# Two units of layer 2 run ahead in the scores' banks, block 1's last units move in front of block 0's last sums, and layer 2's seven products add up in PSUM

## The chip, the cores and the metric

One core of one Trainium2 chip runs the whole kernel. The metric is the device time of one execution in microseconds. PE is the matrix engine (TensorE), DVE is VectorE, ACT is ScalarE, SP issues nearly all DMAs.

## What is computed

Three parts in a row, on 4 x 576 = 2304 tokens of width 512 (8 heads of 64), all in fp32 or better:

```python
scores = q @ k.T / sqrt(64); causal softmax; local = a @ v
mem = (phi(q) @ M_prev) / (phi(q) . z_prev + 1e-6)     # phi(x) = elu(x) + 1
x = sigmoid(beta) * mem + (1 - sigmoid(beta)) * local   # attention
x = softplus(x @ w_in) @ w_out                          # layer 1, 512 -> 2048 -> 512
out = relu(x @ w2_in)**2 @ w2_out                       # layer 2, 512 -> 2048 -> 512
```

The weights arrive as float64. Products run on 16-bit halves: each fp32 operand is split into a high and a low part, and one product is three matmuls (high x high, high x low, low x high).

## The kernel before

**Tiling and order.** Attention goes through 18 chunks g of 128 tokens, 8 heads each, in 104 steps (`attn_step`): scores into the two-bank tile `s_ps` (line 342), mask and row maximum on DVE (line 347), exp on ACT (351), split and transpose, then P x V (399) four steps later. Layer 1 goes through 9 blocks kb of 256 tokens (two chunks). Its work is cut into units: `unit_h(kb, fp)` makes 256 of 2048 hidden columns (24 matmuls, lines 502 to 504; softplus on ACT and DVE, lines 506 to 513, result g in two halves), `unit_x(kb, cp, f0, f1)` the second product (lines 519 to 521) for two of four output chunks over hidden chunks f0 to f1. Block 0 uses `unit_xq(0, q)` instead (lines 564 to 566), which adds quarter q of the hidden chunks into two PSUM banks `xacc` held for the whole block. `w` units split one weight piece (lines 480 to 490).

**What sets the order.** The program is written out in order, and a scheduler with a modelled time puts each engine's instructions in a fixed order, by priority (attention's ones raised) and readiness; every engine then works through its list in order. The planner (lines 692 to 740) mixes units into the attention steps: while the attention of block kb runs, it writes out units of earlier blocks up to `lim`, the modelled time of the queue less a reserve `LEAD_NS` (line 700); `unit_time` (654) prices a unit by its matmuls. Line 717 onward builds the queue for block 1: after three quarters of block 0, six h units of block 1 and their partial sums over f 0 to 12 run early; then come h(0,6), h(0,7), xq(0,3), `close` (which ends the pools `mma`, `xac` and `stage`), h(1,6), h(1,7) and the rest of the sums. The tiles g are named by fp, one buffer each.

**After attention** (lines 742 to 767) the rest of the queue runs while layer 2's weights are loaded and split (`w34_to`), then all PSUM pools close and `mm2` opens with eight banks.

**Layer 2.** The first 512 tokens go the plain way: `plain_h(j)` makes 16 chunks of 128 hidden columns (12 matmuls of 512 columns each, lines 793 to 795), `row_tile` the second product (988 to 990). The other seven blocks of 256 tokens (kb = 2 to 8) use seven products in place of eight for a 2x2 block product. `sums_w3` and `sums_w4` make the sums of weight quarters on DVE, `x_parts(kb)` those of the input. `seven_h(kb, q)` makes half of the hidden columns from seven products of 24 matmuls of 128 columns (878 to 880), each in a bank of its own; DVE adds them up in SBUF (886 to 895), ACT applies Relu and Square. `parts` splits the result, `seven_o(kb, which)` does the second product the same way (938 to 940, adds in line 944), `plain_o` without the trick for two blocks. The results of `seven_h(kb, 0)` lie in the upper half of W3 (`RB`), so they can only be written once `sums_w3` has read it.

**Lines touched:** 161 and 583 (buffers of z and of keys 1), 510 (names of g), 700, 735 to 737 (planner), 761 to 772 (the end of layer 1 and the pools), 783 to 802, 868 to 897, 930 to 964, 997 to 1016, 1027 to 1031.

Of the kernel before, what the change touches and what calls it, by code (L numbers as in the profile page):

```python
# [17 lines left out]
P = 128  # L18

LAG = 4  # L20
LEAD_NS = 15000.0
FR = 0.4
# [33 lines left out]
def kernel(  # L56
# [103 lines left out]
    def z_setup():  # L160
        zr = stage.tile([B * H, 2, D], F32, name="zr", bufs=1)
        z16 = stage.tile([B * H, 2, 2, D], F16, name="z16", bufs=1)
        for i in range(2):
            act.dma_start(out=zr[:, i], in_=z_prev.rearrange("b h d -> (b h) d"))
        act.activation(z16[:, 0], zr, AF.Copy)
        dve.tensor_tensor(z16[:, 1], zr, z16[:, 0], ALU.subtract)
        ps = mm.tile([P, 2, B * H], F16, tag="mm", name="zps")
        for t in range(2):
            pe.transpose(ps[:, t], z16[:, t].rearrange("p i d -> p (i d)"), ident[:B * H, :B * H])
        act.activation(zc, ps, AF.Copy)  # L170
# [321 lines left out]
    g_t = {}  # L492

    def unit_h(kb, fp):
# [15 lines left out]
        g = [w1p.tile([P, 2, NB], F16, name=f"g{t}_{fp}") for t in range(2)]  # L510
# [68 lines left out]
    load("k", 1, stage)  # L579
# [116 lines left out]
    for kb in range(1, NBLK + 1):  # L696
        if kb == 1:
            lim = FR * sum(unit_time(u) for u in queue)
        else:
            lim = sum(unit_time(u) for u in queue) - LEAD_NS  # L700
# [16 lines left out]
        if kb == 1:  # L717
            done = 4 - sum(u[0] == "xq" for u in queue)
            if done < 4:
# [14 lines left out]
                queue = out_q + early + [("close",)]  # L734
                if done < 4:
                    new = new[nh:]
                    xs = [("x", kb, c, 2 * nh, NFC) for c in range(NCC // 2)]
# [22 lines left out]

    for n_, u in enumerate(queue):
        run_unit(u)
        w34_to(NPC * (n_ + 1) // nu)
    mm_cm.__exit__(None, None, None)
    pv_cm.__exit__(None, None, None)
    sps_cm.__exit__(None, None, None)
# [5 lines left out]
    mm2 = ctx.enter_context(tc.tile_pool(name="mm2", bufs=8, space=PSUM, reuse_waits="tile"))  # L772
# [10 lines left out]
    def plain_h(j):  # L783
        x = x_t[0]
        new_g(j)
        for h in range(2):
            for i in range(2):
                f = h * HF + j + i
                ps = mm2.tile([P, 512], F32, tag="mm2", name="h2ps")
                for c in range(NCC):  # L790
                    wh, wl = (w[:, c, f * P:(f + 1) * P] for w in W3)
                    xh, xl = (x[:, t * NCC + c] for t in range(2))
                    pe.matmul(ps, wh, xh, start=(c == 0), stop=False)
                    pe.matmul(ps, wh, xl, start=False, stop=False)
                    pe.matmul(ps, wl, xh, start=False, stop=(c == NCC - 1))
# [5 lines left out]
                dve.tensor_copy(hi, r)  # L801
# [66 lines left out]
    def seven_h(kb, q):  # L868
        X = XT[kb % 2]

        def prod(w, x):
            ps = mm2.tile([P, 512], F32, tag="mm2", name="h2ps")
            for i in range(4):
                o = ps[:, i * P:(i + 1) * P]
                for k in range(2):
                    wh, wl = w3_at(w, k, 4 * q + i)
                    xh, xl = (y[:, x, k * P:(k + 1) * P] for y in X)
                    pe.matmul(o, wh, xh, start=(k == 0), stop=False)  # L878
                    pe.matmul(o, wh, xl, start=False, stop=False)  # L879
                    pe.matmul(o, wl, xh, start=False, stop=(k == 1))  # L880
            return ps.rearrange("p (j t) -> p j t", j=4)
# [3 lines left out]
        act.activation(r11, prod(0, 0), AF.Copy)  # L885
        dve.tensor_tensor(r12, prod(3, 4), r11, ALU.add)
        dve.tensor_tensor(r22, prod(4, 5), r12, ALU.add)
        dve.tensor_tensor(r21, prod(2, 6), r22, ALU.add)
        p5 = prod(6, 3)
        dve.tensor_tensor(r22, p5, r22, ALU.add)  # L890
        dve.tensor_tensor(r12, p5, r12, ALU.add)
        act.activation(r[1], r[1], AF.Relu, scale=u2)
        act.activation(r[1], r[1], AF.Square)
        dve.tensor_tensor(r11, prod(1, 1), r11, ALU.add)
        dve.tensor_tensor(r12, prod(5, 2), r12, ALU.add)
# [29 lines left out]
    OB = {}  # L925

# [3 lines left out]
    def seven_o(kb, which):  # L930
        def prod(n):
            gi, wi = PR[n]
            ps = mm2.tile([P, 512], F32, tag="mm2", name="ops")[:, :256]
            for j in range(HF):
# [3 lines left out]
                pe.matmul(ps, gh, wh, start=(j == 0), stop=False)  # L938
                pe.matmul(ps, gh, wl, start=False, stop=False)  # L939
                pe.matmul(ps, gl, wh, start=False, stop=(j == HF - 1))  # L940
            return ps

        def add(o, ps, y):
            dve.scalar_tensor_tensor(o, ps, SO, y, ALU.mult, ALU.add)

        if which == 0:
            OB[kb] = TS[:, :, NB:]
        o = OB[kb]
        o11, o12, o21, o22 = (o[:, i] for i in range(4))
        if which == 0:  # L950
            act.activation(o12, prod(6), AF.Copy, scale=SO)
            add(o21, prod(7), o12)
            p5 = prod(5)
            add(o22, p5, o21)
            add(o12, p5, o12)
            add(o12, prod(3), o12)
            return
        p1 = prod(1)
        act.activation(o11, p1, AF.Copy, scale=SO)
        add(o[:, 1:], p1.rearrange("p (a c) -> p a c", a=1).to_broadcast([P, 3, 256]), o[:, 1:])  # L960
        add(o11, prod(2), o11)
        store(2 * kb, o[:, :2])
        add(o21, prod(4), o21)
# [33 lines left out]
    for j in range(0, HF, 2):  # L997
        plain_h(j)
        w34_to(NPC + 2 * j + 4)
    st2_cm.__exit__(None, None, None)  # L1000
# [14 lines left out]
    for m in range(XB // P):  # L1015
        row_tile(0, m, XB // 2)
    for j in W4A:
        sums_w4(j)
# [8 lines left out]
    for kb in range(K0, NBLK):  # L1027
# [3 lines left out]
        seven_h(kb, 0)  # L1031
# [41 lines left out]
```

## Time and profile before

| | |
|---|---|
| median of 3 runs | 943.59 us (941.1 to 945.34) |
| the profiled execution | 943.42 us, span 941.6 us |
| mean granted PE clock | 0.979 |
| PE busy | 880.2 us, 93% |
| DVE busy | 728.3 us, 77% |
| ACT busy | 613.6 us, 65% |
| DMA queue 1 | 53.3% of 16 engines |

Times in the rows count from the start of the span. A busy PE is not PE at its peak, as matmuls are pipelined. The granted clock is a share of 2.4 GHz: 0.50 is 1.2 GHz. "Idle before, releaser" at the end of a row is how long the engine stood before that instruction and what ended the wait.

### The profile page before, as it was taken

How to read it: one execution, taken by the hardware profiler on the slowest of the kernel's cores; microseconds unless marked ns; L12 is line 12 of the kernel's file. 1: busy time of each engine (PE TensorE's matmuls, PEld its weight loads, DVE VectorE, ACT ScalarE, POOL GpSimd, SP SyncE). 2: the span in 40 equal slices, each digit the busy share in tenths (PEclk: the TensorE clock that was granted, in tenths of full speed). 3: DMA queues.
4: the chain of work that ended last, by engine and by line, in shares of the span. 5: the costliest groups of instructions: out<-in, count | busy, mean ns of one | idle time of the engine just before them, and what ended most of it. 6: DMA issues, size and time to landing. Idle time of an engine off the chain costs nothing.

```text
span 941.6 us, 24682 instructions
## 1 busy us (share of the span) xinstructions
PE 880.2 (93%) x10385; PEld 730.7 (78%) x10394; DVE 728.3 (77%) x1474; ACT 613.6 (65%) x1160; POOL 2.2 (0%) x10
## 2 busy tenths in 40 slices
PE   5757999889999898999999999999999999999997
PEld 3346888679878897899988887444776999999983
DVE  6798999878757676667856699999997998767640
ACT  7977688679769695867958375663266656444530
POOL 0000000000000000000000000000000000000000
PEclk9879899899999999999999999999999999999999
DMA  9999998799876978658845666500000000000001
GB/s 234 205 217 203 223 206 177 133 150 150 130 131 117 144 134 127 116 101 131 136 86 75 171 199 182 178 22 23 24 2 24 2 24 1 25 24 2 24 13 34
DMA packets 285023, 101.24 MB, mean 108 GB/s; under 512 B 248048, under 2 KB 284400, under 8 KB 284912
## 3 DMA queue, kind: packets, MB, share of 16 engines
q1 hardware_dynamic: 284672, 99.65, 53.3%
q8 instruction: 81, 1.33, 0.6%
q14 instruction: 30, 0.25, 0.1%
q10 hardware_dynamic: 240, 0.02, 0.0%
HBM read 48.78 MB, written 4.72 MB: 57 GB/s over the span
## 4 chain that ended last, share of the span: by engine, by line
PE 52%; DVE 22%; ACT 10%; DMA 10%; issue 5%; SPq 0%; ACTq 0%; DVEq 0%
PE h2ps L878 4%; PE h2ps L879 4%; PE h2ps L880 4%; PE hps L503 4%; PE hps L502 4%; DMA rawq<-in_q_dram 4%; PE hps L504 4%; DMA PT<-p 3%; PE ops L940 3%; PE ops L938 3%; PE ops L939 3%; DVE wcv L481 3%; PE s_ps L342 3%; PE xps L520 3%; PE xps L519 3%
## 5 line engine op out<-in xcount | busy, mean ns | idle before, releaser
L502 PE MATMUL hps<-x,W 128*128 128x256 f16 x576 | 157.5, 275 | 3.8 <-DVE spa L509 1.8
L503 PE MATMUL hps<-x,W 128*128 128x256 f16 x576 | 158.1, 275 | 0.5 <-ACT x L545 0.4
L504 PE MATMUL hps<-x,W 128*128 128x256 f16 x576 | 157.8, 275 | 0.0
L520 PE MATMUL xps<-g,W 128*128 128x256 f16 x512 | 138.8, 273 | 2.4 <-DVE g L513 2.4
L519 PE MATMUL xps<-g,W 128*128 128x256 f16 x512 | 137.8, 273 | 3.3 <-ACT g L512 3.3
L521 PE MATMUL xps<-g,W 128*128 128x256 f16 x512 | 138.8, 273 | 0.0
L351 ACT ACTIVATE Pt<-Pt,cs 128x128 f32<-128x128 f32 (+4 forms) x144 | 84.6, 588 | 45.1 <-DVE cs L347 45.0
L342 PE MATMUL s_ps<-KT,qT 128*128 128x128 f16 (+2 forms) x992 | 75.4, 219 | 22.1 <-DVE cs L347 20.8
L375 DVE TENSOR_TENSOR p<-Pt,p 128x512 f16<-128x512 f32 (+2 forms) x100 | 66.5, 665 | 30.0 <-ACT p L374 29.8
L342 PEld LDWEIGHTS <-qT 128*128 128x128 f16 (+1 forms) x992 | 56.2, 103 | 40.3 <-issue 32.6
L347 DVE CUSTOM_DVE_ANT_0 Pt<-s_ps,mask 128x128 f32<-128x128 f32 (+3 forms) x128 | 61.8, 483 | 19.5 <-PE s_ps L342 19.2
L374 ACT ACTIVATE p<-Pt 128x512 f16<-128x512 f32 (+2 forms) x100 | 60.5, 605 | 15.0 <-DMA PT<-p 14.1
L503 PEld LDWEIGHTS <-W 128*128 128x128 f16 x576 | 56.8, 99 | 9.6 <-issue 3.4
L502 PEld LDWEIGHTS <-W 128*128 128x128 f16 x576 | 56.9, 99 | 7.7 <-DVE spa L509 1.1
L504 PEld LDWEIGHTS <-W 128*128 128x128 bf16 x576 | 56.8, 99 | 7.2 <-issue 0.8
L399 PE MATMUL pvt<-V,PT 128*128 128x64 f16 (+1 forms) x1392 | 58.8, 196 | 1.3 <-DMA PT<-p 1.3
L513 DVE TENSOR_TENSOR g<-spa,g 128x512 f16<-128x512 f32 x72 | 49.4, 685 | 11.2 <-ACT g L512 11.0
L509 DVE SCALAR_TENSOR_TENSOR spa<-hps,spa 128x512 f32<-128x512 f32 x72 | 49.4, 686 | 9.5 <-ACT spa L508 9.2
L519 PEld LDWEIGHTS <-W 128*128 128x128 f16 x512 | 50.0, 98 | 8.7 <-issue 3.3
L521 PEld LDWEIGHTS <-W 128*128 128x128 bf16 x512 | 50.1, 98 | 8.1 <-issue 2.7
L399 PEld LDWEIGHTS <-PT 128*128 128x128 f16 (+1 forms) x1392 | 51.2, 103 | 6.1 <-issue 2.1
L520 PEld LDWEIGHTS <-W 128*128 128x128 f16 x512 | 50.1, 98 | 5.2
(248 smaller groups left out, 2564.8 us busy)
## 6 DMA issues: line engine op xcount, KB each, us to landing
wst<-in_moe_w_in_dram SPq DMA_DIRECT2D x32, 512.0 KB, 4.7
wst<-in_moe_w_out_dram SPq DMA_DIRECT2D x32, 512.0 KB, 4.6
rawk<-in_k_dram SPq DMA_DIRECT2D x16, 256.0 KB, 4.2
rawq<-in_q_dram SPq DMA_DIRECT2D x16, 256.0 KB, 4.3
rawv<-in_v_dram SPq DMA_DIRECT2D x16, 256.0 KB, 3.4
out_dram<-T SPq DMA_DIRECT2D x12, 256.0 KB, 2.4
PT<-p SPq DMA_TRANSPOSE x100, 3.5
mraw<-in_M_prev_dram SPq DMA_DIRECT2D x8, 128.0 KB, 4.5
```

The lines of the kernel that those rows point to most:

```text
L342: pe.matmul(o[x * n:(x + 1) * n], qT[g][:, t * H + h, x * n:(x + 1) * n], KT[kb][:, h, a - j * P:e - j * P], start=(t == 0), stop=(t == 1),)
L347: dve.tensor_tensor_reduce(out=pw, in0=view, in1=mw, scale=-0.125, scalar=3.0e38, op0=ALU.add, op1=ALU.min, accum_out=cs[:, 0, h:h + 1],)
L351: act.activation(pf, pf, AF.Exp, bias=cs[:, 0, h:h + 1], scale=-1.0, accum_out=cs[:, 1, h:h + 1],)
L374: act.activation(v16[:, :, 0], p, AF.Copy)
L375: p_lo.append(dve.tensor_tensor(v16[:, :, 1], p, v16[:, :, 0], ALU.subtract).ins.name)
L399: m = pe.matmul(o[r], t[:, o0 + i + y, r], V[kb][:, z, h, :], start=(i == 0 and y + z == 0), stop=(i == nb - 1 and y > 0),)
L502: pe.matmul(o, wh, x[:, c], start=(c == 0), stop=False)
L503: pe.matmul(o, wh, x[:, NCC + c], start=False, stop=False)
L504: pe.matmul(o, wl, x[:, c], start=False, stop=(c == NCC - 1))
L519: pe.matmul(ps, wh, gh, start=(f == f0), stop=False)
L520: pe.matmul(ps, wh, gl, start=False, stop=False)
L521: pe.matmul(ps, wl, gh, start=False, stop=(f == f1 - 1))
```

## The change

Eight edits. (1) `LEAD_LAST`: the reserve is 30000 instead of 15000 ns while the last block's attention runs. (2) z's staging tile and the second chunk of keys lie in the pool `att` instead of `stage`; keys then have a single buffer. (3) g tiles are named by a running count modulo 8. (4) The remaining h units of block 1 are inserted in front of xq(0,3). (5) The first two chunks of layer 2's first product are issued ahead of the last two x units, into the two banks of `s_ps`, whose pool stays open until `plain_h` is done; `mm2` has six banks until then, and `mm3` eight after. (6) In `plain_h` the high half is copied on ACT instead of DVE. (7) `seven_h` and `seven_o` add products in PSUM: bank a takes four products in turn and is copied out after each, c two, b one; the order of the products changes, and `seven_o` does five products in its first call and two in its second. (8) `seven_h(K0, 0)` is issued before the last row tile.

```diff
 LEAD_NS = 15000.0
+LEAD_LAST = 30000.0
 FR = 0.4
...
     def z_setup():
-        zr = stage.tile([B * H, 2, D], F32, name="zr", bufs=1)
+        zr = att.tile([P, H, D], F32, tag="xf", name="zr")[:B * H, :2]
         z16 = stage.tile([B * H, 2, 2, D], F16, name="z16", bufs=1)
...
     g_t = {}
+    hcount = [0]
...
         dve.scalar_tensor_tensor(a, ps, 0.0, a, ALU.max, ALU.add)
-        g = [w1p.tile([P, 2, NB], F16, name=f"g{t}_{fp}") for t in range(2)]
+        slot = hcount[0] % (NFC // 2)
+        hcount[0] += 1
+        g = [w1p.tile([P, 2, NB], F16, name=f"g{t}_{slot}") for t in range(2)]
         g_t[kb, fp] = g
...
     load("q", 0)
-    load("k", 1, stage)
+    load("k", 1)
     load("v", 0)
...
         else:
-            lim = sum(unit_time(u) for u in queue) - LEAD_NS
+            lim = sum(unit_time(u) for u in queue) - (LEAD_LAST if kb == NBLK - 1 else LEAD_NS)
         end = ready_step(kb) if kb < NBLK else s - 1
...
                 queue = out_q + early + [("close",)]
+                at = queue.index(("xq", 0, 3))
+                queue[at:at] = new[nh:]
                 if done < 4:
-                    new = new[nh:]
+                    new = []
                     xs = [("x", kb, c, 2 * nh, NFC) for c in range(NCC // 2)]
...
+    def h2_mm(ps, f):
+        x = x_t[0]
+        for c in range(NCC):
+            wh, wl = (w[:, c, f * P:(f + 1) * P] for w in W3)
+            xh, xl = (x[:, t * NCC + c] for t in range(2))
+            pe.matmul(ps, wh, xh, start=(c == 0), stop=False)
+            pe.matmul(ps, wh, xl, start=False, stop=False)
+            pe.matmul(ps, wl, xh, start=False, stop=(c == NCC - 1))
     for n_, u in enumerate(queue):
+        if n_ == nu - NCC // 2:
+            for f in range(2):
+                h2_mm(s_ps[:, f], f)
         run_unit(u)
...
     pv_cm.__exit__(None, None, None)
-    sps_cm.__exit__(None, None, None)
     w1_cm.__exit__(None, None, None)
...
     bp = bp_cm.__enter__()
-    mm2 = ctx.enter_context(tc.tile_pool(name="mm2", bufs=8, space=PSUM, reuse_waits="tile"))
+    mm2_cm = tc.tile_pool(name="mm2", bufs=6, space=PSUM, reuse_waits="tile")
+    mm2 = mm2_cm.__enter__()
     u2 = S_R / S_X2
...
     def plain_h(j):
-        x = x_t[0]
         new_g(j)
...
                 f = h * HF + j + i
-                ps = mm2.tile([P, 512], F32, tag="mm2", name="h2ps")
-                for c in range(NCC):
-                    wh, wl = (w[:, c, f * P:(f + 1) * P] for w in W3)
-                    xh, xl = (x[:, t * NCC + c] for t in range(2))
-                    pe.matmul(ps, wh, xh, start=(c == 0), stop=False)
-                    pe.matmul(ps, wh, xl, start=False, stop=False)
-                    pe.matmul(ps, wl, xh, start=False, stop=(c == NCC - 1))
+                if f < 2:
+                    ps = s_ps[:, f]
+                else:
+                    ps = mm2.tile([P, 512], F32, tag="mm2", name="h2ps")
+                    h2_mm(ps, f)
                 r = bp.tile([P, 512], F32, name="r2", bufs=3)
...
                 r = r.rearrange("p (a t) -> p a t", a=2)
-                dve.tensor_copy(hi, r)
+                act.activation(hi, r, AF.Copy)
                 dve.tensor_tensor(lo, r, hi, ALU.subtract)
...
-        def prod(w, x):
-            ps = mm2.tile([P, 512], F32, tag="mm2", name="h2ps")
+        def prod(ps, w, x, first, last):
             for i in range(4):
...
                     xh, xl = (y[:, x, k * P:(k + 1) * P] for y in X)
-                    pe.matmul(o, wh, xh, start=(k == 0), stop=False)
-                    pe.matmul(o, wh, xl, start=False, stop=False)
-                    pe.matmul(o, wl, xh, start=False, stop=(k == 1))
-            return ps.rearrange("p (j t) -> p j t", j=4)
+                    s = first and i == 0 and k == 0
+                    pe.matmul(o, wh, xh, start=s, stop=False, skip_group_check=True)
+                    pe.matmul(o, wh, xl, start=False, stop=False, skip_group_check=True)
+                    pe.matmul(o, wl, xh, start=False, stop=last and i == 3 and k == 1, skip_group_check=True)
+        def bank():
+            ps = mm2.tile([P, 512], F32, tag="mm2", name="h2ps")
+            return ps, ps.rearrange("p (j t) -> p j t", j=4)
...
         r11, r12, r21, r22 = r[0][:, 0], r[0][:, 1], r[1][:, 0], r[1][:, 1]
-        act.activation(r11, prod(0, 0), AF.Copy)
-        dve.tensor_tensor(r12, prod(3, 4), r11, ALU.add)
-        dve.tensor_tensor(r22, prod(4, 5), r12, ALU.add)
-        dve.tensor_tensor(r21, prod(2, 6), r22, ALU.add)
-        p5 = prod(6, 3)
-        dve.tensor_tensor(r22, p5, r22, ALU.add)
-        dve.tensor_tensor(r12, p5, r12, ALU.add)
-        act.activation(r[1], r[1], AF.Relu, scale=u2)
+        (a, a4), (b, b4), (c, c4) = bank(), bank(), bank()
+        prod(a, 0, 0, True, True)
+        act.activation(r11, a4, AF.Copy)
+        prod(c, 6, 3, True, True)
+        prod(a, 3, 4, False, True)
+        act.activation(r12, a4, AF.Copy)
+        prod(b, 1, 1, True, True)
+        dve.tensor_tensor(r11, b4, r11, ALU.add)
+        prod(a, 4, 5, False, True)
+        act.activation(r22, a4, AF.Copy)
+        dve.tensor_tensor(r22, c4, r22, ALU.add)
+        prod(a, 2, 6, False, True)
+        act.activation(r21, a4, AF.Relu, scale=u2)
+        act.activation(r22, r22, AF.Relu, scale=u2)
         act.activation(r[1], r[1], AF.Square)
-        dve.tensor_tensor(r11, prod(1, 1), r11, ALU.add)
-        dve.tensor_tensor(r12, prod(5, 2), r12, ALU.add)
+        prod(c, 5, 2, False, True)
+        dve.tensor_tensor(r12, c4, r12, ALU.add)
         act.activation(r[0], r[0], AF.Relu, scale=u2)
...
     OB = {}
+    AC = {}
...
     def seven_o(kb, which):
-        def prod(n):
+        def prod(ps, n, first):
             gi, wi = PR[n]
-            ps = mm2.tile([P, 512], F32, tag="mm2", name="ops")[:, :256]
             for j in range(HF):
...
                 wh, wl = w4_at(wi, j)
-                pe.matmul(ps, gh, wh, start=(j == 0), stop=False)
-                pe.matmul(ps, gh, wl, start=False, stop=False)
-                pe.matmul(ps, gl, wh, start=False, stop=(j == HF - 1))
-            return ps
-        def add(o, ps, y):
-            dve.scalar_tensor_tensor(o, ps, SO, y, ALU.mult, ALU.add)
+                pe.matmul(ps, gh, wh, start=(first and j == 0), stop=False, skip_group_check=True)
+                pe.matmul(ps, gh, wl, start=False, stop=False, skip_group_check=True)
+                pe.matmul(ps, gl, wh, start=False, stop=(j == HF - 1), skip_group_check=True)
+        def bank():
+            return mm2.tile([P, 512], F32, tag="mm2", name="ops")[:, :256]
+        def copy(o, ps):
+            act.activation(o, ps, AF.Copy, scale=SO)
+        def add(o, ps):
+            dve.scalar_tensor_tensor(o, ps, SO, o, ALU.mult, ALU.add)
...
             OB[kb] = TS[:, :, NB:]
+            AC[kb] = bank(), bank()
+        a, c = AC[kb]
         o = OB[kb]
...
         if which == 0:
-            act.activation(o12, prod(6), AF.Copy, scale=SO)
-            add(o21, prod(7), o12)
-            p5 = prod(5)
-            add(o22, p5, o21)
-            add(o12, p5, o12)
-            add(o12, prod(3), o12)
-            return
-        p1 = prod(1)
-        act.activation(o11, p1, AF.Copy, scale=SO)
-        add(o[:, 1:], p1.rearrange("p (a c) -> p a c", a=1).to_broadcast([P, 3, 256]), o[:, 1:])
-        add(o11, prod(2), o11)
+            prod(a, 1, True)
+            copy(o11, a)
+            prod(c, 5, True)
+            prod(a, 6, False)
+            copy(o12, a)
+            b = bank()
+            prod(b, 2, True)
+            add(o11, b)
+            prod(a, 7, False)
+            copy(o22, a)
+            add(o22, c)
+            return
+        prod(c, 3, False)
+        add(o12, c)
         store(2 * kb, o[:, :2])
-        add(o21, prod(4), o21)
+        prod(a, 4, False)
+        copy(o21, a)
         store(2 * kb + 1, o[:, 2:])
...
         w34_to(NPC + 2 * j + 4)
+    mm2_cm.__exit__(None, None, None)
+    sps_cm.__exit__(None, None, None)
+    mm2 = ctx.enter_context(tc.tile_pool(name="mm3", bufs=8, space=PSUM, reuse_waits="tile"))
     st2_cm.__exit__(None, None, None)
...
     x_parts(K0 + 1)
-    for m in range(XB // P):
+    for m in range(XB // P - 1):
         row_tile(0, m, XB // 2)
+    seven_h(K0, 0)
+    row_tile(0, XB // P - 1, XB // 2)
     for j in W4A:
...
             x_parts(kb + 1)
-        seven_h(kb, 0)
+        if kb > K0:
+            seven_h(kb, 0)
         if K0 < kb <= K0 + NPL:
...
```

## Rows read from the trace of the kernel before

**Rows 1.** The page's first part: busy time, share and instructions of each engine.
```profile
PE 880.2 (93%) x10385; PEld 730.7 (78%) x10394; DVE 728.3 (77%) x1474; ACT 613.6 (65%) x1160; POOL 2.2 (0%) x10
```

**Rows 2.** Busy time by stage; the columns stand in the first line.
```profile
core 0: us, PE busy (x) PEld busy (x) DVE busy (x) ACT busy (x) POOL busy (x), PEclk, DMA share, GB/s
205.00:525.00 320.00, 311.38 (x4292) 277.09 (x4290) 222.30 (x509) 248.84 (x523) 0.00 (x0) 1.00 0.72 120
525.00:576.00 51.00, 49.15 (x450) 43.74 (x448) 44.14 (x80) 29.53 (x50) 0.00 (x0) 1.00 0.64 192
589.00:629.00 40.00, 40.00 (x187) 18.13 (x186) 39.90 (x81) 25.83 (x48) 0.00 (x0) 1.00 0.37 116
670.00:726.00 56.00, 54.07 (x695) 42.86 (x696) 51.44 (x78) 31.12 (x39) 0.00 (x0) 1.00 0.03 11
726.00:916.00 190.00, 190.00 (x2595) 180.31 (x2594) 144.27 (x225) 99.44 (x124) 0.00 (x0) 1.00 0.05 16
```

**Rows 3.** PE's waits, 205 to 916 us: total us, times, longest.
```profile
PE s_ps L342 <- DVE cs L347: 6.1, 5, 2.4
...
PE hps L503 <- ACT x L545: 0.4, 1, 0.4
```

**Rows 4.** Busy time in steps of 5 us, 165 to 205 us, columns as above.
```profile
175.00:180.00 5.00, 4.19 (x41) 3.27 (x39) 5.00 (x12) 3.19 (x8) 0.00 (x0) 0.50 0.41 54
180.00:185.00 5.00, 5.00 (x68) 4.45 (x67) 3.10 (x8) 3.36 (x8) 0.00 (x0) 0.89 0.47 84
...
195.00:200.00 5.00, 2.46 (x26) 1.79 (x23) 3.58 (x9) 5.00 (x12) 0.00 (x0) 0.81 1.10 203
200.00:205.00 5.00, 5.00 (x67) 4.34 (x66) 2.61 (x5) 2.62 (x6) 0.00 (x0) 0.85 1.13 145
sum 40.00, PE 32.22 PEld 27.19 DVE 30.36 ACT 27.27 POOL 0.00; mean PE 4.03 PEld 3.40 DVE 3.80 ACT 3.41 POOL 0.00
```

**Rows 5.** Timeline, 172 to 198 us: start, duration, instruction, idle before and releaser.
```profile
172.53 0.28 PE L564 MATMUL xacc<-g,W 128*128 128x256 f16 x1 [2.22 <-ACT W L489]
177.49 0.68 DVE L513 TENSOR_TENSOR g<-spa,g 128x512 f16<-128x512 f32 x1
184.68 1.24 SPq L223 DMA_TRANSPOSE x<-xn  x1
198.00 0.50 PE L519 MATMUL xps<-g,W 128*128 128x256 f16 x2 [2.54 <-ACT g L512]
```

**Rows 6.** Timeline of PE at the last units of layer 1.
```profile
574.01 0.38 PE L519 MATMUL xps<-g,W 128*128 128x256 f16 x2 [0.48 <-ACT g L512]
575.76 0.27 PE L520 MATMUL xps<-g,W 128*128 128x256 f16 x1 [1.36 <-DVE g L513]
575.86 0.27 PE L521 MATMUL xps<-g,W 128*128 128x256 f16 x1
```

**Rows 7.** Timeline of SP: the first issues of layer 2's weights.
```profile
528.84 2.25 SPq L461 DMA_DIRECT2D wst<-in_moe_w_in_dram  x4
```

**Rows 8.** Timeline of one seven_h product and its evacuation.
```profile
898.65 0.22 PE L878 MATMUL h2ps<-XT,W 128*128 128x128 f16 x1
...
899.94 0.22 PE L880 MATMUL h2ps<-XT,W 128*128 128x128 f16 x1
...
900.20 0.60 ACT L885 ACTIVATE r<-h2ps 128x512 f32<-128x512 f32 x1 [2.02 <-PE h2ps L880]
...
901.61 0.69 DVE L886 TENSOR_TENSOR r<-h2ps,r 128x512 f32<-128x512 f32 x1 [2.33 <-PE h2ps L880]
```

**Rows 9.** Timeline of PE in the second and third seven-product unit.
```profile
689.90 0.23 PE L878 MATMUL h2ps<-XT,W 128*128 128x128 f16 x1 [1.77 <-ACT W L897]
```

**Rows 10.** Line 347's instructions, 205 to 916 us: ns min/median/max, first and last start.
```profile
L347 DVE DVE_READ_ACCUMULATOR2_ANT cs<- x86: 80/83/85, 206.2 to 516.6; 128x1 f32 x86
```

**Rows 11.** Timeline of the start: split of keys 0, and of queries 1.
```profile
5.78 0.69 DVE L257 TENSOR_TENSOR kn<-rawk,kn 128x512 f16<-128x512 f32 x1 [1.00 <-ACT kn L256]
...
19.06 0.63 ACT L237 ACTIVATE qn<-rawq 128x512 f16<-128x512 f32 x1
```

## The prediction

> **What bounds the kernel now.** I read the page's totals first, then the busy time by stage, then PE's waits stage by stage. PE is busy for 880.2 of 941.6 us, more than any other engine [rows 1], and from 205 us on it is nearly full: 311.4 of 320 us while attention and layer 1 run side by side (205 to 525 us), and 190.0 of 190 in the seven-product part of layer 2 (726 to 916 us) [rows 2]. So an engine other than PE can get much lighter there and the end doesn't move. What an edit can win is PE's idle time and PE's slow time, and both sit in few places. From 205 to 916 us PE's waits come to 12.3 us over seven lines of the view, of which the first, for the scores' banks, is half and the last 0.4 us [rows 3]. Between 165 and 205 us it stood still for 40.00 - 32.22 = 7.78 us, and part of what it did run there ran at a low clock: granted 0.50 from 175 to 180 us, that is 1.2 GHz, after 2.22 us of standing still just before [rows 4, 5]. The first 160 us hold more idle time, but the change leaves their order alone except for one load.
>
> The profiled execution took 943.42 us with a span of 941.6, so 1.8 us lie around it. The median is 943.59. I subtract from 943.42.
>
> **Block 1's last units in front of block 0's last sums.** Before, the order after block 1's first twelve f is h(0,6), h(0,7), xq(0,3), close, h(1,6), h(1,7), x(1,0,12..16). The sums xq(0,3) had to wait: its instruction at 172.53 us came 2.22 us late, behind ScalarE's split of a layer-1 weight piece, and the last half of its g, written by line 513, began only at 177.49 [rows 5]. Work that could have filled this, h(1,6) and h(1,7), stood behind it. Then those two ran, and the product x(1,0,12..16) that needs them stood directly behind: 2.54 us of waiting at 198.00 for g (line 512) [rows 5]. The change turns this around. Two units of 24 products, at the 0.11 us between 256-wide products seen in [rows 6], are 24 x 2 x 0.11 = 5.3 us of PE work that slides from behind the sums into their wait. The weights they need (f 12 to 15 of W1) are the same that h(0,6) and h(0,7) have just used. With slots counted by hcount, h(1,6) and h(1,7) take slots 6 and 7, last held by h(1,0) and h(1,1), whose readers, the partial sums, stand earlier in the queue. The second wait goes because g of h(1,7) is then made while xq(0,3) runs.
>
> What this is worth: at most all idle time, 7.78 us, and all slow time. Slow time is busy time times the missing clock: 4.19 x 0.50 + 5.00 x 0.11 + 2.46 x 0.19 + 5.00 x 0.15 = 2.10 + 0.55 + 0.47 + 0.75 = 3.9 us [rows 4]. So the bounds are 0 and -11.7 us. I take the two waits (2.22 + 2.54 = 4.8) and 60% of the slow time (2.3), because without the hole at 170 us the fall in clock behind it has no cause left: **-7.0 us**. Not all of it, because block 2's last input is only transposed from 184.68 us on [rows 5], so PE may stand for a moment after xq. A gain here carries through to the end, since PE is the bound from 205 us on and the unit list behind is long enough.
>
> **LEAD_LAST.** The planner holds 30 instead of 15 us of units back while the last block's attention runs. Worked out with its own unit_time, 70.7 instead of 52.4 us of units are left when attention is over. Three more h units and x(7,0) stand behind attention instead of beside it. Attention ends earlier by about that difference, and layer 2's weights, first issued at 528.84 us [rows 7], start some 15 to 18 us sooner. VectorE, which is full from 525 on (44.1 of 51 us, then 39.9 of 40) [rows 2], gets a head start. PE wins nothing by it directly, as it was full. The cost: attention with thinner filling. In the 320 us of [rows 2] PE lost 320 - 311.4 = 8.6 us over seven blocks' attention, 1.2 us each; with thinner filling I take as much again, **+1 us**. Ends: 0, and 4.8, two waits of 2.4 us, the longest seen there [rows 3].
>
> **Two layer-2 units ahead, in s_ps.** PE waited 0.48 and 1.36 us for the last g of layer 1 [rows 6]; behind that gap plain_h started. Twenty-four 512-wide products now stand in front of the last two x units, without a need for that g: 24 times at least 0.11 us, so over 2.6 us of cover for 1.84 us of waiting. They need the first two W3 pieces, which by the counting in the queue loop are split long before. **-1.8 us**, ends 0 and -1.8. The price is six banks instead of eight for plain_h; ScalarE reads each bank in 0.60 us [rows 8], so six are plenty.
>
> **plain_h's hi copies on ScalarE.** Sixteen 128x512 copies: about 16 x 0.6 = 9.6 us more on ScalarE, priced by the nearest row, its 0.60 us read of a bank [rows 8], and at most 16 x 0.69 = 11 us less on VectorE [rows 8]. ScalarE is busy 25.8 of 40 us there [rows 2], so it has room, and PE is full. Nothing on the path, but it lets the sums of W3 and W4 end earlier.
>
> **seven_h(K0,0) before the last row tile.** At 689.90 PE waited 1.77 us in the second and third seven-product units [rows 9], while VectorE, busy 51.4 of 56 us there, was behind with the sums of W4 and the parts [rows 2]. With the head start, the lighter evacuation and a row tile's 48 products put behind the first unit, VectorE is no longer late: **-1.8 us**, ends 0 and -1.8.
>
> **Layer 2's products add up in PSUM.** In each of the 14 seven_h units, four VectorE adds of 0.69 us go, two ScalarE copies of 0.60 come [rows 8] and one Relu is cut in two halves. In seven_o four of a block's seven VectorE adds go and two ScalarE copies come. PE's products are the same in number and shape. As PE is full in 726 to 916, this wins nothing by itself. It adds waits on PE, which had none there: a product may be added to bank a only after ScalarE has copied a. A product is 24 matmuls, 898.65 to about 900.0 us, 1.35 us; the copy starts 0.2 us after its end and lasts 0.60 [rows 8], so the link costs PE about 0.85 us if nothing stands between. Three links have a whole product in between and are hidden. The fourth, between prod(a,4,5) and prod(a,2,6), has nothing. In list order the unit behind is the block before's seven_o (for K0 the last row tile), whose first twelve products need only parts that are long ready, 12 x 0.11 = 1.3 us; the schedule can slip them in. Ends: 0 and 14 x 0.85 = 11.9 us. The nearest row is another link of PE to an evacuation with filler beside it, the scores' banks: 6.1 us lost [rows 3] over 86 of them [rows 10], 0.07 us each. All 56 links at that rate give 4 us, only the 14 tight ones 1 us: **+2 us**.
>
> The Trainium skill speaks against this edit (Perfetto Trace Analysis, Matmuls): independent groups of matmuls should rotate through different banks, so that one's evacuation lies beside the next one's products. Before, each product had its own bank; after, three serve seven. By that rule the uncovered link would be paid, which is the first rival below.
>
> **The load of keys 1.** rawk has one buffer in att, so chunk 1's keys, which had a buffer of their own in stage, now wait for the split of chunk 0's, which ended at 6.47 us. What stands behind them on SP, the values, M and the first weight pieces, may pass them and come a little sooner. Keys 1 are of use only together with chunk 1's queries, which were split at 19.06 us [rows 11], 12 us after the load can start. **0**, ends -1 and +1, about one such split of 0.69 us on either side. z_setup's other buffer changes no order.
>
> **Sum.** 943.42 - 7.0 + 1 - 1.8 - 1.8 + 2 + 0 = **935.8 us**.
>
> **Rivals.**
> 1. *The bank link is paid (slower).* Place: seven_h, between prod(a,4,5) and prod(a,2,6). Without filling, 14 x 0.85 = 11.9 instead of 2: 945.7 us. With one more ScalarE instruction of 0.60 ahead of the copy, 14 x 1.45 = 20 us: 954. For it: [rows 2] show PE without a hole, every wait is new. Against it: the scores' links, well filled. The change stops being a gain at (7.65 + 2) / 14 = 0.69 us per unit. Chance 0.12.
> 2. *The waits only move (no change).* Attention, not PE, paces 165 to 205 us: VectorE is full from 175 to 180 us [rows 4]. Then h(1,6) and h(1,7) run earlier and PE waits the same sum elsewhere. 935.8 + 7 = 943, or 941 if part is kept. For it: two h units more put load on a full VectorE. Against it: VectorE is idle for over a quarter of the time from 195 to 200 us, where the longest wait is. Chance 0.26.
> 3. *All of it.* With the full 11.7 us and free links: 929. It lies in the forecast's own range.
>
> **How the numbers follow.** Forecast with rival 3: 0.62, range 927 to 939. Rival 2: 0.26, 939 to 945. Rival 1: 0.12, 945 to 954. Range for 8 in 10: 927 to 945. About 0.5% is what a measurement of this kernel can tell from no change, 938.9 and 948.3 us: faster 0.63, same 0.28, slower 0.09.
>
> **What would show it.** Right: no wait over 1 us on lines 519 and 564 of layer 1 between 165 and 205 us, and a clock of 1.00 there; no wait at the last x units; seven_h without a hole before prod(a,2,6), filled by ops products; layer 2's weights issued before 515 us. Wrong: PE waiting for ScalarE in seven_h more than 2 us in all, new score waits in the last block, or the same idle sum at 165 to 205 us.

## The result, and the profile after

| | before | after |
|---|---|---|
| median, 4 runs each | 944.47 us (941.10 to 946.89) | 935.10 us (933.93 to 935.45) |
| ratio, 95% interval | | 0.9909 (0.9887 to 0.9930) |
| the profiled execution | 943.42 us, span 941.6 (the profile ahead of the prediction) | 935.16 us, span 933.4 |

The change takes 0.9% off, about 8.6 us. The forecast of 935.8 us is met. As the experiments show, several of its terms were not: they cancelled, so that the number is in part luck.

The page's first part, answering [rows 1]:

```profile
PE 878.1 (94%) x10394; PEld 730.1 (78%) x10394; DVE 683.9 (73%) x1382; ACT 641.4 (69%) x1228; POOL 2.2 (0%) x10
```

PE has the same work in a shorter span. 44 us left VectorE and 28 us came to ScalarE, which by itself says nothing of the time.

Busy time by stage, answering [rows 2]:

```profile
core 0: us, PE busy (x) PEld busy (x) DVE busy (x) ACT busy (x) POOL busy (x), PEclk, DMA share, GB/s
205.00:525.00 320.00, 311.09 (x4259) 275.65 (x4257) 221.04 (x506) 245.02 (x518) 0.00 (x0) 0.99 0.72 123
525.00:576.00 51.00, 51.00 (x446) 43.41 (x444) 48.56 (x87) 30.46 (x52) 0.00 (x0) 1.00 0.66 199
...
670.00:726.00 56.00, 56.00 (x715) 43.98 (x712) 41.65 (x61) 35.45 (x51) 0.00 (x0) 1.00 0.05 16
726.00:916.00 190.00, 190.00 (x2497) 176.13 (x2495) 105.44 (x152) 111.50 (x159) 0.00 (x0) 1.00 0.05 16
```

The holes of 525 to 576 us (49.15 busy before) and of 670 to 726 us (54.07) are closed. From 205 to 525 us nothing was won: 311.09 against 311.38.

Steps of 5 us around the edited queue, and their sum from 165 to 205 us, answering [rows 4]:

```profile
175.00:180.00 5.00, 4.56 (x68) 3.96 (x66) 5.00 (x12) 4.87 (x11) 0.00 (x0) 1.00 0.57 87
...
185.00:190.00 5.00, 3.70 (x63) 3.42 (x62) 5.00 (x10) 5.00 (x12) 0.00 (x0) 1.00 0.83 159
...
sum 40.00, PE 37.02 PEld 33.51 DVE 34.45 ACT 31.64 POOL 0.00; mean PE 4.63 PEld 4.19 DVE 4.31 ACT 3.96 POOL 0.00
```

PE stands still for 2.98 us in place of 7.78, and the granted clock is 1.00 in all eight steps, where it had fallen to 0.50.

PE's waits from 205 to 916 us (total, times, longest), answering [rows 3]:

```profile
PE s_ps L343 <- DVE cs L348: 3.8, 5, 1.4
PE hps L504 <- DMA x<-xn: 3.1, 1, 3.1
PE nps L303 <- DVE spa L511: 0.7, 1, 0.7
PE s_ps L343 <- DMA KT<-kn: 0.5, 1, 0.5
PE pvt L391 <- DVE xt L426: 0.3, 1, 0.3
PE h2ps L893 <- ACT W L905: 0.2, 1, 0.2
```

The second line is new: one wait of 3.1 us for the next block's transposed input. The last is the only wait in `seven_h` for a bank used again. Behind the new wait the granted clock falls, from 1.00 (2.4 GHz) to 0.52, close to the 0.50 that is 1.2 GHz:

```profile
315.00:320.00 5.00, 1.79 (x25) 1.36 (x25) 2.34 (x9) 2.52 (x8) 0.00 (x0) 0.80 0.99 202
320.00:325.00 5.00, 5.00 (x28) 3.68 (x27) 3.46 (x9) 2.38 (x6) 0.00 (x0) 0.52 0.45 70
```

The busy time in these two rows, times the missing clock, is 2.8 us. Before, the clock was 1.00 in every step from 205 to 400 us.

### The profile page after: what moved, and what is told of

The parts are those of the page before. It is cut to its first block, busy times and chain, and to the rows that moved or that the text cites. A ratio compares the mean times of both kernels' runs of the same rounds, so it can differ in the third digit from the quotient of the medians.

```text
span 933.4 us, 24615 instructions
## 1 busy us (share of the span) xinstructions
PE 878.1 (94%) x10394; PEld 730.1 (78%) x10394; DVE 683.9 (73%) x1382; ACT 641.4 (69%) x1228; POOL 2.2 (0%) x10
## 4 chain that ended last, share of the span: by engine, by line
PE 65%; DVE 13%; DMA 9%; ACT 8%; issue 3%; SPq 1%; ACTq 0%; DVEq 0%
PE xps L524 5%; PE xps L523 5%; PE xps L525 5%; PE h2ps L893 5%; PE h2ps L895 5%; PE h2ps L894 5%; PE hps L505 4%; PE hps L504 4%; PE hps L506 4%; PE ops L964 3%; PE ops L962 3%; PE ops L963 3%; PE s_ps L343 3%; DMA PT<-p 3%; PE pvt L400 2%
## 5 line engine op out<-in xcount | busy, mean ns | idle before, releaser
L348 DVE CUSTOM_DVE_ANT_0 Pt<-s_ps,mask 128x128 f32<-128x128 f32 (+3 forms) x128 | 62.0, 484 | 22.9 <-PE s_ps L343 20.2
L504 PEld LDWEIGHTS <-W 128*128 128x128 f16 x576 | 57.1, 99 | 11.4 <-DMA x<-xn 3.3
L505 PEld LDWEIGHTS <-W 128*128 128x128 f16 x576 | 57.0, 99 | 6.6
L490 ACT ACTIVATE W<-wcv 128x512 f16<-128x512 f32 x56 | 35.0, 625 | 34.9 <-DVE wcv L483 34.8
L517 DVE TENSOR_TENSOR g<-spa,g 128x512 f16<-128x512 f32 x72 | 49.3, 686 | 12.6 <-ACT g L516 12.4
L523 PEld LDWEIGHTS <-W 128*128 128x128 f16 x512 | 50.1, 98 | 5.5
```

Of the source, the lines that this page charges most:

```text
L348: dve.tensor_tensor_reduce(out=pw, in0=view, in1=mw, scale=-0.125, scalar=3.0e38, op0=ALU.add, op1=ALU.min, accum_out=cs[:, 0, h:h + 1],)
L504: pe.matmul(o, wh, x[:, c], start=(c == 0), stop=False)
L505: pe.matmul(o, wh, x[:, NCC + c], start=False, stop=False)
L523: pe.matmul(ps, wh, gh, start=(f == f0), stop=False)
```

## How the traces are compared

A wait that goes in one place can come back in another, so I sum PE's losses by stage: over all 5-us rows of the view of busy time, idle time (5 less busy) plus slow time (busy times the missing clock). In us:

| stage | before | after | after, run again (e5) | move alone (e1) | reserve alone (e12) | both (e11) | all but move (e2) |
|---|---|---|---|---|---|---|---|
| 0 to 160 | 46.2 | 51.0 | 43.3 | 46.6 | 45.0 | 48.5 | 46.5 |
| 160 to 205 | 11.8 | 3.0 | 2.8 | 4.1 | 10.1 | 2.5 | 8.6 |
| 205 to 400 | 8.4 | 10.3 | 7.9 | 12.4 | 6.9 | 12.3 | 8.5 |
| 400 to 525 | 0.2 | 1.4 | 0.9 | 0.8 | 0.2 | 1.2 | 0.2 |
| 525 to 580 | 1.8 | 0 | 0 | 2.9 | 3.9 | 1.8 | 0 |
| 670 to 730 | 1.9 | 0 | 0 | 0.2 | 0 | 0 | 0 |

The first row is a warning: the same kernel lost 51.0 us there in one profile and 43.3 in another. So a single span can't tell a few microseconds, and the verdicts below go by ratios to the kernel before, measured together with it on the same chip. e1 to e4 ran together and e5 to e8 together, on one chip; e9 to e11 ran together and e12 by itself, on another. The chip of the result is not on record.

## Experiments

**e1, the queue move alone.** The kernel before with edits 3 and 4:

```diff
+                at = queue.index(("xq", 0, 3))
+                queue[at:at] = new[nh:]
                 if done < 4:
-                    new = new[nh:]
+                    new = []
```

> The kernel before with the queue move alone (g named by a running count, the last two h units of block 1 in front of block 0's last sums). The theory of the forecast: the waits of 2.22 and 2.54 us at the last sums and at the rest of block 1's product go, and with them the low clock from 175 to 185 us; in the changed kernel idle plus slow PE time between 160 and 205 us fell from 11.8 to 3.0 us. So this kernel is 5 to 9 us faster than the one before, about 937 us where that takes 944. The rival (the waits only move, attention sets the pace there): less than 2.5 us faster, with the same idle sum between 160 and 320 us.

945.11 us, ratio 1.0019 (0.9999 to 1.0038): nothing won. Yet at 160 to 205 us the loss fell from 11.8 to 4.1 us as it should. From 160 to 320 us the sum is nearly the same (14.2 us, and 15.1 before), as the rival had it; from 160 to 400 us it is 16.4 against 20.2. Of the 7.7 us won, 4.0 came back between 205 and 400 us, 3.5 of them slow time, of which the kernel before has none there, then 1.1 at the last x units, and some in a place where no view of idle time shows it. PE is "busy" all through 500 to 510 us; its timeline there (start, duration):

```profile
504.53 0.28 PE L505 MATMUL hps<-x,W 128*128 128x256 f16 x1
504.74 0.22 PE L342 MATMUL s_ps<-KT,qT 128*64 128x64 f16 x1
504.89 0.28 PE L503 MATMUL hps<-x,W 128*128 128x256 f16 x1
...
506.37 0.28 PE L504 MATMUL hps<-x,W 128*128 128x256 f16 x1
506.58 0.24 PE L342 MATMUL s_ps<-KT,qT 128*64 128x128 f16 x1
506.75 0.28 PE L505 MATMUL hps<-x,W 128*128 128x256 f16 x1
...
507.53 0.28 PE L504 MATMUL hps<-x,W 128*128 128x256 f16 x1
507.65 0.22 PE L342 MATMUL s_ps<-KT,qT 128*128 128x128 f16 x1
507.71 0.27 PE L505 MATMUL hps<-x,W 128*128 128x256 f16 x1
```

One score product of 128*64 between two h products makes a pair last 0.38 us (506.37 to 506.75). One of 128*128 with as many columns makes it 0.18 (507.53 to 507.71). Half the array's width thus costs 0.2 us more when it alternates singly with full width. It isn't slow as such: in the changed kernel 22 such products in a row take 0.70 us up to the h product behind them.

```profile
506.38 0.87 PE L343 MATMUL s_ps<-KT,qT 128*64 128x128 f16 x22
507.08 0.27 PE L506 MATMUL hps<-x,W 128*128 128x256 f16 x1
```

Sixteen score products stand singly between h products in e1: 16 x 0.2 = 3.2 us. Measured as work (each product at the rate of its back-to-back runs) against time, 460 to 525 us lost 4.7 us more than in the kernel before.

**e2, everything but the move.** The changed kernel with edit 4 undone.

> The changed kernel with the queue move undone (h(1,6), h(1,7) behind the close again); all else as changed. If the move is worth 5 to 9 us here too, this kernel takes 940 to 944 us where the changed one takes 935, and shows the two waits of over 2 us and a clock near 0.5 around 175 us again. If the gain of the change came from the other edits (last units, layer 2), it stays within 2 us of 935.

936.86 us, ratio 0.9957 (0.9931 to 0.9983), against 0.9909 (0.9887 to 0.9930) and 0.9891 (0.9866 to 0.9916) with the move. In company the move is worth 0.5 to 0.65%, with intervals that barely part (0.9931 and 0.9930), though alone it was worth nothing.

**e3, keys 1 and z back in `stage`.** The changed kernel with edit 2 undone.

> The changed kernel with z's tile and the second chunk of keys in the pool stage again, as before the change. In the changed kernel the first 160 us lost 51.0 us of PE to idle and slow time, before the change 46.3. If the single key buffer (and the order of loads that follows from it) is the cause, this kernel has the start of the kernel before, the first h unit at about 69 instead of 72 us, and ends 2 to 5 us sooner, 930 to 933 us. If that loss is hidden, since attention is paced later anyway, it stays within 1 us of 935.

937.98 us, ratio 0.9953 (0.9932 to 0.9975): slower than with edit 2, outside both expectations. The load isn't what does it: the first scores start at 12.0 us, and at 11.9 in the changed kernel. The trace has 11.7 us lost from 205 to 400 us and one wait of 1.9 us at 680 us in `seven_h` (line 893, for ScalarE), like that of [rows 9]. Why edit 2 is worth 0.4% stays open; that it shifts the scheduler's order elsewhere is a guess.

**e4, without the larger reserve.** The changed kernel with `LEAD_LAST = 15000.0`.

> The changed kernel with a reserve of 15 instead of 30 us in the last block. The forecast priced the larger reserve at +1 us and gave it no gain of its own, so this kernel would take 934 us, within 1 us. The rival: the earlier start of layer 2's weights and the head start it gives VectorE are what took the wait of 1.77 us out of the second and third seven-product unit; then a wait of 1 to 2 us is back between 670 and 726 us, or one in front of the seven-product units, and this kernel takes 936 to 938 us.

934.35 us, ratio 0.9923 (0.9900 to 0.9946): not told apart from the full change. In its trace 14 half-width score products stand singly between h products near 500 us, and 460 to 525 us loses about 3 us more, measured as work, than in the runs with the reserve. Beside all the other edits the reserve is thus worth 0.1 to 0.3% (against the result and e5), which can't be told from nothing.

**e5, the change again**, unaltered, measured together with e6 to e8.

> The changed kernel once more, unaltered, as the measure beside which the kernels with one part undone stand, on the same chip: 935 us within 1.5 us.

930.65 us, ratio 0.9891 (0.9866 to 0.9916), against 0.9909 in the result, with overlapping intervals and 4 us below what was expected: this is the mark for e6 to e8.

**e6, edits 5 to 8 alone** (reserve and queue as before).

> The kernel before with only the edits behind attention: two layer-2 units ahead in the scores' banks, high halves copied on ScalarE, products added up in PSUM, the first seven-product unit before the last row tile. Queue move, reserve, keys and z as before. The move alone gained nothing (1.0019), though it emptied the waits between 160 and 205 us: PE waited more from 205 to 320 us, where the next block's attention was not earlier. If that is the whole story, the end edits carry the change: rows give 1.8 us at the last units of layer 1 and 1.9 us between 670 and 730 us, so 939 us if only the waits count, and 935 to 937 us if layer 2 gains more than its waits. The rival, that the move gains in company of the other edits: 940 us or more here.

938.34 us, ratio 0.9970 (0.9952 to 0.9988), -2.8 us. The waits at the last x units and at 690 us are gone, 11.3 us are lost at 160 to 205 us as before.

**e7, the seven products summed on VectorE again**, in a bank each; all else of the change stays.

```diff
-        prod(a, 3, 4, False, True)
-        act.activation(r12, a4, AF.Copy)
+        dve.tensor_tensor(r12, prod(3, 4), r11, ALU.add)
```

> The changed kernel with the old seven_h and seven_o: each product in its own bank, sums on VectorE, evacuation as before. If the adding up in PSUM is what keeps VectorE from being late, the wait in the second and third seven-product unit (1.77 us before) is back, and this kernel takes 936 to 938 us. If the head start in time and the row tile between are enough, there is no wait over 0.5 us from 670 us on and it takes what the changed kernel takes, 935 us. If the bank links cost PE something, it is faster than the changed one, by up to 2 us.

929.83 us, ratio 0.9884 (0.9863 to 0.9905), against 0.9891: no difference, though the intervals leave room for 2 to 3 us. Adding up in PSUM took 41 us off VectorE (724.3 to 683.7) and put 18 on ScalarE (622.7 to 640.9), on two engines that have room, and PE has no wait from 525 to 916 us in either.

**e8, nothing runs ahead.** The two units of layer 2 are made in `plain_h` again:

```diff
-        if n_ == nu - NCC // 2:
-            for f in range(2):
-                h2_mm(s_ps[:, f], f)
...
                     ps = s_ps[:, f]
+                    h2_mm(ps, f)
```

> The changed kernel without the run-ahead: the first two units of layer 2 are made in plain_h, still in the scores' banks, behind the last units of layer 1. The forecast: PE's waits of 0.48 and 1.36 us for the last g come back, 1.8 us in all, 937 us. The rival: with three more h units between attention and the end VectorE is less late, the waits are below 0.5 us, and the time stays at 935.

931.08 us, ratio 0.9898 (0.9875 to 0.9921): no difference that can be told. PE's waits at the last x units came back only as 0.5 us.

**e9, nothing may fill the links.** The changed kernel with an order on PE alone: no product of `seven_o`, `plain_o` or the last row tile may be issued before the last product of the `seven_h` unit written ahead of it.

```diff
+            tc.add_manual_dep(m.ins, sh_last[-1], mybir.DependencyInfo(
+                mybir.DependencyClass.NoSync, mybir.DependencyReason.DATA), reason="no filler")
```

> The changed kernel, with an order on PE alone: no product of seven_o, plain_o or the last row tile may be put between the products of a seven_h unit; each unit's last product must have been issued first. Nothing is left out or added in work. What is tested is the price of a bank that is added to again when nothing else may fill the wait. Rival 1 (the link costs what was worked out): PE waits for ScalarE before prod(a,2,6) about 0.85 us in each of the 14 units, 11.9 us in all; PE busy from 726 to 916 us falls from 190.0 to about 179, and the time rises to 942 to 947 us where the changed kernel has 931 to 935, ratio 0.999 to 1.003 to the kernel before. If a link costs nothing even bare (the copy is done by the time the next product's weights are loaded): no waits there, ratio 0.989 to 0.992. In between, waits of 0.4 us each: 937 to 940 us.

953.79 us, ratio 1.0128 (1.0104 to 1.0152), 21 to 22 us above the change by the ratios, and above the 942 to 947 us expected. The timeline at the first link, and busy time from 726 to 916 us:

```profile
655.49 0.22 PE L906 MATMUL h2ps<-XT,WS 128*128 128x128 f16 x1
655.75 0.60 ACT L924 ACTIVATE W<-h2ps 128x512 f32<-128x512 f32 x1 [1.59 <-PE h2ps L906]
656.40 0.22 PE L902 MATMUL h2ps<-XT,W 128*128 128x128 f16 x1 [0.69 <-ACT W L924]
...
726.00:916.00 190.00, 181.04 (x2440) 170.02 (x2437) 102.19 (x147) 103.16 (x150) 0.00 (x0) 1.00 0.04 13
```

From 655.49 to 656.40 is 0.91 us where 0.06 is the rhythm: 0.85 us for a bare link, exactly what rival 1 had worked out. All 14 units show it: 0.69 us of idle time in ten of them, up to 1.56 in the others, 11.1 us together. Five more waits stand before the third product on bank a (line 920's copy, 4.9 us). PE's waits add up to 17 us, and the 0.16 us that each of the 20 longer ones costs beside its idle time (0.85 - 0.69) make it 20. The same link in the changed kernel:

```profile
755.54 0.22 PE L895 MATMUL h2ps<-XT,WS 128*128 128x128 f16 x1
755.59 0.27 PE L964 MATMUL ops<-WT,GA 128*128 128x256 f16 x1
...
755.79 0.60 ACT L912 ACTIVATE r<-h2ps 128x512 f32<-128x512 f32 x1 [0.86 <-PE h2ps L895]
756.90 0.27 PE L964 MATMUL ops<-WT,GA 128*128 128x256 f16 x1
757.01 0.22 PE L893 MATMUL h2ps<-x,W 128*128 128x128 f16 x1
```

Thirteen products of `seven_o` stand in the gap (755.59 to 756.90) while ScalarE copies, and none waits. The Trainium skill (Perfetto Trace Analysis, Matmuls) wants independent groups of matmuls to rotate through different banks for this overlap. With nothing else to run, e9 bears the rule out, at 0.85 us a link; where another group's products fill the gap, e5 and e7 show no wait and no difference that can be told.

**e10, a larger reserve in the other blocks too.** The changed kernel with

```diff
-LEAD_NS = 15000.0
+LEAD_NS = 25000.0
```

> The changed kernel with LEAD_NS 25000 instead of 15000 while blocks 1 to 7 are attended (the last block keeps 30000). What is tested is whether what the move gave back at 205 to 320 us is PE running out of units. In the changed kernel PE waits 3.1 us at 315.5 us for the transposed input of the next block (line 504), and idle and slow time from 205 to 320 us is 7.8 us where the kernel before had 3.2. If PE had run out because attention was too late, with 10 us more held back attention comes sooner per unit of fill, the wait at 315 us goes, idle from 205 to 320 falls to 3 to 5 us, and the time falls by 3 to 4 us: ratio 0.985 to 0.988. If attention itself paces this stretch (the reserve only moves the place of the waits), the waits turn into waits for the scores' banks with the same sum, 7 to 9 us, and the ratio stays 0.989 to 0.992 or gets worse.

943.11 us, ratio 1.0013 (0.9996 to 1.0030): the whole gain is gone. PE's waits from 110 to 400 us:

```profile
PE s_ps L343 <- DVE cs L348: 6.9, 7, 2.0
PE nps L303 <- DMA phiT<-phin: 6.4, 5, 3.2
PE pvt L391 <- DVE xt L426: 3.4, 2, 3.0
...
PE hps L504 <- DMA x<-xn: 0.5, 1, 0.5
```

The 3.1 us at line 504 went and attention's own waits took its place: 14.9 us lost from 205 to 400 us against 10.3, and 6.1 against 3.0 just before. Up to 320 us the units held back didn't make attention sooner (block 4's input was transposed at 316.1 us, against 314.6 in the changed kernel); they left PE without filling inside it. Only later did attention run ahead (its last input at 514.5 against 520.2 us), too late to make up for that.

**e11 and e12, the square of two edits.** The kernel before with edits 1, 3 and 4, and with edit 1 alone:

```diff
-            lim = sum(unit_time(u) for u in queue) - LEAD_NS
+            lim = sum(unit_time(u) for u in queue) - (LEAD_LAST if kb == NBLK - 1 else LEAD_NS)
```

> The kernel before with three of the eight edits: g tiles by a running count, h(1,6) and h(1,7) in front of xq(0,3), and LEAD_LAST 30000. The move alone left the time where it was (ratio 1.0019), with 11.8 us of idle and slow time at 160 to 205 us turned into 4.1, but 3 us lost again near 505 us, where score products of half width alternate with products of the h units one by one, and 2.9 us at the last x units; in company it is worth about 0.5% (0.9957 without it, 0.9909 with it). If the loss at the end of layer 1 is what ate the move's gain, and the larger reserve takes it away, this kernel comes out near 0.994 to 0.996, with less than 1 us of waits at the last x units or with no alternation at 500 to 516 us. If the gain is given back between 205 and 320 us whatever stands behind, it stays at 0.999 to 1.003.

> The kernel before with LEAD_LAST 30000 alone. It completes the square of two edits: neither 1.000, the move alone 1.0019, the move and the larger reserve 0.9941. Theory: the reserve has nothing to win by itself, since in the kernel before no score product of half width alternates with products of the h units; it only takes away the 3 to 5 us that the alternation cost beside the move. Then this kernel is at 0.997 to 1.001, with 11 to 12 us of idle and slow time at 160 to 205 us as before, no alternation at 500 to 520 us, and the times of the square don't add up. Rival: the reserve itself brings the gain (layer 2's weights come sooner, VectorE has a head start, the wait of 1.77 us at 690 us goes): 0.993 to 0.996, and the move is worth nothing.

| | queue as before | queue moved |
|---|---|---|
| reserve 15 | 1 | 1.0019 (0.9999 to 1.0038) |
| reserve 30 in the last block | 0.9989 (0.9973 to 1.0005) | 0.9941 (0.9918 to 0.9964) |

Neither edit does anything that can be told alone; together they take 0.6% off. In e1 sixteen half-width products stand singly between h products from 495 to 508 us; in e11 there are three, far apart, and in e12 none there. That, and 1.1 us less at the last x units, covers 4 to 6 of the 7 us between e1 and e11. What the move gives back hangs on one wait. The transposes of block 4's input on SP, before and after, and PE after:

```profile
311.92 1.47 SPq L223 DMA_TRANSPOSE x<-xn  x1
```

```profile
314.59 1.55 SPq L224 DMA_TRANSPOSE x<-xn  x1
...
318.60 0.39 PE L504 MATMUL hps<-x,W 128*128 128x256 f16 x1 [3.10 <-DMA x<-xn]
```

Before, block 4's first product came at 323.1 us, long after its input. After the move PE is early (block 3's first product comes at 262.3 instead of 268.4 us, block 4's at 318.6), has used up its units and waits for attention. e1 and e11 show the same wait, 4.3 and 3.9 us long. All nine kernels with the move and the old reserve in the middle blocks have it, 2.8 to 4.3 us, with 1.4 to 3.5 us of slow time from 205 to 400 us; the four without the move have neither.

## Why the forecast held, step by step

| term | forecast, us | the runs |
|---|---|---|
| move of the queue | -7.0 (0 to -11.7) | -4.5 beside the reserve (0.9941 against 0.9989), +1.8 alone (1.0019) |
| `LEAD_LAST` | +1 (0 to 4.8) | -1.0 alone (interval past 0), -7 beside the move (0.9941 against 1.0019), -1 to -3 beside everything (e4, not told apart) |
| run ahead, `seven_h` earlier, PSUM | -1.8 - 1.8 + 2 = -1.6 | -2.8 (0.9970) |
| keys 1 | 0 (±1) | load 0; edit 2 as a whole about -4 (e3), cause open |

**The move** was right in its place and mechanism. Nine kernels with it (all but e10, where the reserve differs) lost 2.5 to 4.1 us at 160 to 205 us (mean 3.1), four without it 8.6 to 11.8 (mean 10.5). That is -7.4, the forecast's -7.0, and the clock stayed at 1.00 in the changed kernel, as said. The step that failed is "A gain here carries through to the end, since PE is the bound from 205 us on and the unit list behind is long enough". In the same thirteen kernels 205 to 400 us lost 10.2 us with the move (7.9 to 12.4) and 7.9 without (6.9 to 8.5): 2.3 us given back, a third of the gain. PE is full there, but with units that run ahead of attention, and at 315 us they run out. So rival 2 had a true cause (attention paces) at the wrong place: not at 165 to 205 us, but a hundred microseconds on. Its price was another, too. The idle time alone is 8.0 us with the move and 7.9 without, so the sum of the waits didn't grow; one of them became long, and what was given back is slow time, most of it behind that wait (2.3 us on average, against 0.0). The forecast had counted the low clock at 175 us as gone for good; part of it only moved.

**The reserve** was mis-sized, and beside the move mis-signed. I priced thinner filling at +1 us; the last block showed no wait at all from 460 to 525 us (65.00 of 65 busy after). e10 shows that the fear itself was sound: with a reserve of 25 us in the blocks before the last it cost about 10 us (1.0013 against 0.9891 to 0.9909). What the reserve brought beside the move was not in the sum: an order of the last block without the half-width alternation. Beside all the other edits it brought 1 to 3 us, not told from nothing (e4). That layer 2's weights start before 515 us held in one profile (513.9 in e5) and not in the other (521.4 after); the 15 to 18 us forecast from the planner's times were 7.4 and 15.0.

**Run ahead and `seven_h(K0, 0)`.** Both waits are gone after, as forecast. But e8 gives back 0.5 us of 1.8 at the x units, and the wait of [rows 9] is gone in e11 and e12 too (0.2 us in e1), which have neither edit, and is back in e3 (1.9 us), which has both. So for the two terms the size of the group is shown (-2.8 with PSUM), and which edit of it earned what is not.

**Sums in PSUM** was mis-sized as far as the traces tell: +2 forecast, 0.2 us of waits after and none in e5; the times of e5 and e7 alone can't tell 2 us. Rival 1's price was right at ten of the 14 links, its condition (no filling) wasn't met; e9 made it so. Its 14 links paid 11.1 + 14 x 0.16 = 13.3 us, near the 11.9; most of the rest is the link before. That the time, 953.8, meets the rival's upper end of 954 is chance, since that was worked out from other terms.

So the forecast landed at 935.8 partly by luck: a move 2.5 us too large was balanced by a bank cost 2 us too high and by a reserve and an edit 2 that seem to have won where I had them lose or do nothing. The parts don't add up either: e11 gives -5.6 us, e6 -2.8 and edit 2 by e3 about -4, together -12, where the change takes 8.6 to 10.3 (e5).

## What to carry to other kernels

Follow a gain on the fullest engine to the next place where it depends on another chain: PE that is early runs out of work there and gives part back, here as a low clock behind one long wait. Reusing a bank is free as long as another group's products lie ready to fill the copy, and costs the whole round trip when they don't. Test edits of one schedule together as well as alone, since a reserve worth nothing by itself was worth 0.8% here beside one edit, and 0.1 to 0.3%, not told from nothing, beside all of them.

## What was not expected of the hardware

Switching between half-width (128*64) and full-width products costs time that shows as busy: 0.38 us for a pair against 0.18 with full width and the same columns, so 0.1 us per switch, and 3.2 us for 16 such pairs. The Trainium skill (TensorEngine Tiling (Array Packing), Key Properties) says that a change of tiling mode drains TensorE; the rows of e1 fit that and give a price; the drain itself is not seen in them. And a wait on a bank costs PE more than the idle time that the view shows: 0.85 us for 0.69 us of idle. The rest is arithmetic of the rows: the last product before the wait is shown as 0.22 us long, while products back to back start 0.06 us apart, and 0.22 - 0.06 = 0.16.
